# Forming weight sums two steps ahead, beside another block's products

## The chip, the cores and the metric

The kernel runs on one core of a Trainium2 chip. Its time is device microseconds of one execution; the number to compare is the median of several runs. Engines are named as in the profile: PE is TensorE's matmul, PEld its weight load, DVE VectorE, ACT ScalarE, POOL GpSimd, SP SyncE, which here issues nearly all DMA transfers.

## The reference

Retention (linear attention with a decay for each head) is followed by a layer of two matrix products with an activation between them. Batch 8, 8 heads, 576 positions, head size 64; the result of the attention, 4608 tokens x 512, goes through weights of 512 x 2048 and 2048 x 512, all in float32.

```python
scores = (q @ k.T) / sqrt(64)                  # per batch and head
ret = scores * where(i >= j, gamma[h] ** (i - j), 0)
x = (ret @ v).transpose(0, 2, 1, 3).reshape(4608, 512)
h = x @ w_in                                   # first products
g = h - tanh(h)
out = g @ w_out                                # second products
```

## The kernel before, in words

The sequence is cut into 9 chunks of 64 positions. A chunk of all 8 batches is a block of 512 columns (block n is chunk n). The attention of a block works in pairs of batches, with a running state for each batch and head, in small 64x64 matmuls. The 2048 middle features are 16 slices `f` of 128.

Every float32 operand of a large product is split in two words, a high word that ACT makes by rounding (`gh`, `xh`, `wi` and so on, in the type fp32r) and a low word that DVE makes by subtracting the high one (`gl`, `xl`). A product is then three matmuls: high x high, high x low, low x high. A first product of one slice is 12 matmuls (`mm1`, line 434), and so is a second product of one slice (`mm2`, line 489).

The order of work:

- Blocks 0 and 1 do their first products while the weights are being loaded and split. Their h goes to DRAM (`spill`).
- The late loop (line 686) does the second products of block 1 and then of block 0, 31 steps of 12 matmuls in the loop and one behind it. In step k, `words` splits g of step k + 1 (ACT `gh` at line 471, DVE `gl` at line 472), `resume` makes g of step k + 2 (ACT tanh at line 464, DVE subtraction `s` at line 465), and `fetch` loads step k + 4 from DRAM. In steps 3, 16 and 29 `entry3` does attention for block 2; it is followed by loads of its next operands on SP and their scaling on POOL (`prep`, line 240). Steps 7 and 20 have such a load and scaling too.
- Block 2 does its first products (line 972), its g going to DRAM by `spill`, and then its second products (`stage_b`), between which stands the attention of blocks 3 and 4 (`attend`).
- Blocks 3 to 8 go in pairs. For the two blocks of a pair and two slices f1, f2 of the first weights, eight half products are made from seven by a scheme of sums and differences (`stage_a`, `product`). The seven operands on the weights' side, variants 0 to 6 for each of 8 pairs j of slices, lie in DRAM (`wvar`, 56 entries of 256 KB). Three of them (0, 5, 6) are parts of the weights as they are, the raw words; four (1 to 4) are sums and differences, which `variants(j)` makes: four operations on POOL (lines 835 to 839), then on DVE ta (line 840) and tb (line 841), a cast of each on ACT (line 843), a low word of each on DVE (line 844) and two stores on SP (line 845).

`attend` (line 766) has its matmuls write the attention of two batches to the PSUM bank `own`, and makes from it the words of the seven operands on the side of x. `put(v, b, src, 0)` is a high word on ACT (line 760), `put(v, b, src, 1)` a low word on DVE (line 762). For the first block of a pair ACT also copies the bank to `a` in SBUF (line 790), for the second block to `own` in SBUF (line 802).

Each engine carries out its instructions in the order of the program (`in_order`); nothing is moved by a planner. A buffer with one tag is reused in turn; `xh1` and `xl1` are the words of x of block 1, which nothing reads once its first products are done. `xl1` also holds the result of block 1 on its way out in step 15 of the late loop. g has three buffers, `gh` and `gl` two each, `own` one bank.

Of the kernel before, what the change touches and what calls it, by code (L numbers as in the profile page):

```python
# [9 lines left out]
F32 = mybir.dt.float32  # L10
F32R = mybir.dt.float32r
# [3 lines left out]
ALU = mybir.AluOpType  # L15
# [4 lines left out]
P = 128  # L20
NF = DF // P
# [14 lines left out]
NV = 7  # L36
# [35 lines left out]
def retention_ffn(ctx: ExitStack, tc: tile.TileContext, ins, out, spill, wvar):  # L72
    nc = tc.nc
    first_d, krows_d, qkv_d, w_in, w_out, qtab_d, vtab_d, mask_d, decay_d = ins

    const = ctx.enter_context(tc.tile_pool(name="const", bufs=1))
    pool = ctx.enter_context(tc.tile_pool(name="pool", bufs=2))
# [7 lines left out]
    win, wout, wraw, masks = {}, {}, {}, {}  # L85

    def place(t, f):
        return "wi1" if (t, f) == ("i", 14) else f"w{t}{f}"
# [141 lines left out]
    def prep(j, t, n=2):  # L230

        if j >= NI:
            return
        c = j // B
        a = parts[j, t][:, :, 0]
        if t == 0:
            table = qtabs[c].unsqueeze(1).broadcast_to([P, n, 4, C])
        else:
            table = vtab[:, c].unsqueeze(1).unsqueeze(3).broadcast_to([P, n, 4, D])
        nc.gpsimd.tensor_tensor(a, a, table, op=ALU.mult)  # L240
# [86 lines left out]
    def bank(name, tag):  # L327
        return psp.tile([P, 2, 4, D], F32, tag=tag, bufs=2 if tag == "h" else 1, name=name)
# [5 lines left out]
    def pair(what, j, bank):  # L334
        return what(j, bank[:, 0]) + what(j + 1, bank[:, 1])
# [121 lines left out]
    def fetch(n, f):  # L457
        fetched[n, f] = pool.tile([P, BLK], F32, tag="g", bufs=3, name=f"s{n}_{f}")
        nc.sync.dma_start(fetched[n, f], spill[n, f])

    def resume(n, f):
        g = fetched[n, f]
        th = pool.tile([P, BLK], F32, tag="cv", bufs=4, name=f"th{n}_{f}")
        nc.scalar.activation(th, g, AF.Tanh)
        nc.vector.tensor_tensor(g, g, th, op=ALU.subtract)

    def words(n, f):
        g = fetched.pop((n, f))
        gh = pool.tile([P, BLK], F32R, tag="gh", name=f"gh{n}_{f}")
        gl = pool.tile([P, BLK], F32R, tag="gl", name=f"gl{n}_{f}")  # L470
        nc.scalar.copy(gh, g)
        nc.vector.tensor_tensor(gl, g, gh.bitcast(F32), op=ALU.subtract)
        gs[n, f] = (gh, gl)
# [110 lines left out]
    for j in range(B):  # L584
        o = psp.tile([P, 8, C], F32, tag=("o2", "o3", "own")[j % 3], bufs=1, name=f"own_first{j}")[:, :4]
# [50 lines left out]
    for k, (n, f) in enumerate(seq):  # L636
# [32 lines left out]
        if k in early:  # L669
            p = early[k]  # L670
# [8 lines left out]
    def raw_words(f):  # L679

        j, w = f // 2, win[f].bitcast(F32)
        for v, cc in ((0, 0), (5, 2)) if f % 2 == 0 else ((6, 2),):
            nc.sync.dma_start(wvar[:, NV * j + v].rearrange("p (s m) -> p s m", s=2), w[:, :, cc : cc + 2].rearrange("p s c m -> p s (c m)"))

    rest = []
    for k, (n, f) in enumerate(late):
        if k in (3, 16, 29):
            follow = entry3(first + (0, 2, 5)[(3, 16, 29).index(k)], rest)
        if 0 < k < len(late) - 1:
            words(*late[k + 1])  # L690
        if k < len(late) - 2:
            resume(*late[k + 2])
        if k + 4 < len(late):
            fetch(*late[k + 4])
        if k in (3, 16, 29):

            follow()
        if k in (7, 20):
            load_part(rest[0], 0)
            prep(rest.pop(), 0)  # L700
        if k >= NF:
            raw_words(k - NF)
        for _ in range(2 if k < 4 else 1):
            step()
        if k < len(late) - 1:
            mm2(n, f)
# [2 lines left out]

    turns = [(c + u) * B + b for c in range(FIRST, NC, 2) for b in range(0, B, 2) for u in range(2)]  # L710
    work = pool.tile([P, 4, DM], F32, tag="xl1", bufs=1, name="work")

    def place_of(f):
        return place("i", f) if f != 1 else "wi14"

    def load_tables(c):

# [38 lines left out]
    def put(v, b, src, sub):  # L756

        hi, lo = [x[:, :, b * C : (b + 2) * C].rearrange("p i (u t) -> p u i t", u=2) for x in xv[v]]
        if sub == 0:
            nc.scalar.copy(hi, src)  # L760
        else:
            nc.vector.tensor_tensor(lo, src, hi.bitcast(F32), op=ALU.subtract)  # L762
# [3 lines left out]
    def attend(m, between):  # L766

        j = turns[m]
        c, b = divmod(j, B)
        first, states = (c - FIRST) % 2 == 0, c < NC - 1  # L770
        if first and b == 0:
            new_xv()
        o = bank(f"own{j}", "own")
        outs, same = pair(m_out, j, o), []
        if states:
            new = bank(f"new{j}", "new")
            same += pair(m_state, j, new)
        more = m + 1 < len(turns)
        if more:
            sc = bank(f"s{turns[m + 1]}", "h")  # L780
            same = pair(m_score, turns[m + 1], sc) + same
        run(same, outs)
        if more:
            after_score(turns[m + 1], sc, 2)
        if first:
            a = pool.tile([P, 2, 4, C], F32, tag="cv", bufs=4, name=f"xa{j}")
            kept[b] = a
            put(0, b, o[:, :, 0:2], 0)
            put(5, b, o[:, :, 2:4], 0)
            nc.scalar.copy(a, o)  # L790
            if states:
                add_state(j, new)
            between()
            put(0, b, o[:, :, 0:2], 1)
            put(5, b, o[:, :, 2:4], 1)
        else:
            a = kept.pop(b)
            t13 = pool.tile([P, 2, 2, 2, C], F32, tag="cv", bufs=4, name=f"t13_{j}")
            t24 = pool.tile([P, 2, 2, 2, C], F32, tag="cv", bufs=4, name=f"t24_{j}")
            t1, t3, t2, t4 = t13[:, 0], t13[:, 1], t24[:, 0], t24[:, 1]  # L800
            own = pool.tile([P, 2, 4, C], F32, tag="cv", bufs=4, name=f"xb{j}")
            nc.scalar.copy(own, o)
            put(4, b, o[:, :, 2:4], 0)
            nc.vector.tensor_tensor(t3, own[:, :, 2:4], own[:, :, 0:2], op=ALU.subtract)
            nc.gpsimd.tensor_tensor(t2, t3, a[:, :, 0:2], op=ALU.add)
            nc.vector.tensor_tensor(t1, own[:, :, 0:2], a[:, :, 0:2], op=ALU.subtract)
            nc.gpsimd.tensor_tensor(t4, a[:, :, 2:4], t2, op=ALU.subtract)
            if states:
                add_state(j, new)
            put(3, b, t3, 0)  # L810
            put(2, b, t1, 0)
            between()
            put(4, b, o[:, :, 2:4], 1)
            put(3, b, t3, 1)
            put(2, b, t1, 1)
            put(1, b, t2, 0)
            put(6, b, t4, 0)
            put(1, b, t2, 1)
            put(6, b, t4, 1)
        prep_turn(m + 2, 0)  # L820
        prep_turn(m + 1, 1)
        load_turn(m + 3, 0)
        load_turn(m + 2, 1)


    def variants(j):

        f1, f2 = [win[2 * j + u].bitcast(F32) for u in range(2)]
        r1, r2, ta, tb = [pool.tile([P, 2, 2, P], F32, tag="cv", bufs=4, name=f"{n}{j}") for n in ("r1", "r2", "ta", "tb")]
        if j == 0:  # L830
            ots = [pool.tile([P, 2, 2, 2, P], F32R, tag="xh1", bufs=1, name=f"ot{j}_{u}") for u in range(2)]
        else:
            ots = [const.tile([P, 2, 2, 2, P], F32R, tag=place_of(2 * j - 2 + u), name=f"ot{j}_{u}") for u in range(2)]
        for r, f in ((r1, f1), (r2, f2)):
            nc.gpsimd.tensor_tensor(
                r.rearrange("p k c m -> p (k c) m"), f[:, 0], f[:, 1], op=ALU.add,
            )
        nc.gpsimd.tensor_tensor(ta[:, 1], r2[:, 0], r2[:, 1], op=ALU.add)
        nc.gpsimd.tensor_tensor(tb[:, 0], r1[:, 0], r2[:, 0], op=ALU.subtract)
        nc.vector.tensor_tensor(ta[:, 0], ta[:, 1], r1[:, 0], op=ALU.subtract)  # L840
        nc.vector.tensor_tensor(tb[:, 1], r1[:, 1], ta[:, 0], op=ALU.subtract)
        for u, t in enumerate((ta, tb)):
            nc.scalar.copy(ots[u][:, :, 0], t)
            nc.vector.tensor_tensor(ots[u][:, :, 1], t, ots[u][:, :, 0].bitcast(F32), op=ALU.subtract)  # L844
            nc.sync.dma_start(
                wvar[:, NV * j + 1 + 2 * u : NV * j + 3 + 2 * u], ots[u].bitcast(F32).rearrange("p v s c m -> p v (s c m)"),
            )

    slots = {}
    per = NV * NPAIR // 4  # L850
# [121 lines left out]
    for f in range(NF):  # L972
        mm1(2, f)
        if f == 0:
            mm2(*late[-1])
        if f % 2 == 1:
            variants(f // 2)
        if f == 8:
            load_turn(1, 0)
            load_turn(2, 0)  # L980
            load_turn(1, 1)
        if f == 11:
            prep_turn(1, 0)
# [68 lines left out]
```

## Time and profile before

| | us |
|---|---|
| median of 3 runs (884.51 to 888.09) | 887.48 |
| the profiled execution | 886.59 |
| its span | 884.8 |
| PE busy in the span | 851.0 |
| DVE busy | 491.2 |
| ACT busy | 340.6 |
| POOL busy | 188.2 |

Times in views of the trace are from the start of the span. In a row of the timeline come the start, the duration, the engine, the line, the operation, what it writes and reads, the shapes and the count of instructions merged; brackets give how long the engine stood idle before it and what ended that. Matmuls overlap: a row of four takes 1.07 us, but the next begins 0.91 us after it. A row of the list of waits says which engine at which line waited for which, the total, the number of times and the longest.

### The profile page before, as it was taken

Reading aid. Unit: us, or ns where it says so; the run is one execution under the profiler, and the core shown is the slowest. Engines: PE = TensorE matmul, PEld = TensorE weight load, DVE = VectorE, ACT = ScalarE, POOL = GpSimd, SP = SyncE. Lnnn points to the kernel's source line nnn. Section 1 sums busy time; section 2 is a strip of 40 time slices with the busy share of each in tenths; the row PEclk is TensorE's granted clock in tenths of the full one; section 3 lists DMA queues with packets and bytes.
Section 4 is the critical chain, followed back from the end, with each engine's and each line's share of the span. In section 5 each row is a group of like instructions: output and inputs, shape, how many; then the busy total and the mean of one; then the engine's idle time right before and its main releaser. Section 6 shows DMA issues by size and latency. Waiting matters only on the chain.

```text
span 884.8 us, 18546 instructions
## 1 busy us (share of the span) xinstructions
PE 851.0 (96%) x7701; PEld 699.6 (79%) x7702; DVE 491.2 (56%) x742; ACT 340.6 (38%) x633; POOL 188.2 (21%) x165
## 2 busy tenths in 40 slices
PE   7999999999786999999999999999999999999997
PEld 6788888878664777888888878888887888888886
DVE  5899876544575576544445766344447744343421
ACT  5887754443233232322233333222233333232221
POOL 0000001010673243211132343121115312121100
PEclk9999999999897999999999999999999999999999
DMA  8967945586588747644467646444476445442442
GB/s 319 365 232 252 350 137 179 164 294 199 183 300 312 282 144 213 206 166 143 167 206 221 219 164 213 161 163 146 167 238 199 139 134 174 169 153 109 118 122 71
DMA packets 72580, 174.54 MB, mean 197 GB/s; under 512 B 7472, under 2 KB 14896, under 8 KB 67120
## 3 DMA queue, kind: packets, MB, share of 16 engines
q1 hardware_dynamic: 71968, 172.44, 58.4%
q8 instruction: 60, 0.98, 0.4%
q10 hardware_dynamic: 528, 0.92, 0.3%
q14 instruction: 24, 0.20, 0.1%
HBM read 124.57 MB, written 48.76 MB: 196 GB/s over the span
## 4 chain that ended last, share of the span: by engine, by line
PE 84%; DMA 7%; DVE 4%; ACT 2%; issue 2%; POOL 0%; SPq 0%; ACTq 0%; DVEq 0%; POOLq 0%
PE o L489 25%; PE o L900 15%; PE h L434 12%; PE pnew L869 7%; PE pv L869 7%; PE pown L869 4%; PE py L869 4%; PE pz L869 4%; DMA s<-spill_dram 3%; PE own L290 3%; PE s L290 3%; PE new L290 2%; DMA spill_dram<-g 1%; DVE ot L844 1%; DMA qk<-in_qkv_dram 1%
## 5 line engine op out<-in xcount | busy, mean ns | idle before, releaser
L489 PE MATMUL o<-wo,gh 128*128 128x512 f32 x608 | 158.2, 398 | 8.5 <-ACT gh L884 7.6
L489 PEld LDWEIGHTS o<-wo,gh 128*128 128x128 f32 x608 | 113.8, 190 | 34.6 <-ACT gh L884 8.0
L923 POOL TENSOR_TENSOR c<-c,th 128x512 f32<-128x512 f32 x48 | 62.1, 1296 | 269.1 <-ACT th L919 267.9
L434 PE MATMUL h<-xh,wi 128*128 128x512 f32 x384 | 100.3, 397 | 9.0 <-DVE g L452 7.8
L919 ACT ACTIVATE th<-c 128x512 f32<-128x512 f32 x72 | 45.5, 632 | 148.5 <-DVE c L933 97.4
L434 PEld LDWEIGHTS h<-xh,wi 128*128 128x128 f32 x384 | 71.6, 190 | 27.4 <-DVE g L452 10.4
L489 PE MATMUL o<-wo,gl 128*128 128x512 f32 x304 | 85.0, 392 | 0.0
L900 PE MATMUL o<-wo,gs 128*128 128x512 f32 x288 | 70.6, 389 | 0.0
L240 POOL TENSOR_TENSOR vr<-vr,vtab 128x512 f32<-128x512 f32 x27 | 32.1, 1192 | 172.4 <-DMA vr<-in_qkv_dram 79.6
L489 PEld LDWEIGHTS o<-wo,gl 128*128 128x128 f32 x304 | 57.6, 190 | 12.2
L900 PEld LDWEIGHTS o<-wo,gs 128*128 128x128 f32 x288 | 54.1, 188 | 11.2
L290 PE MATMUL own<-qk,state 64*64 64x64 f32 x928 | 57.6, 221 | 3.1 <-DVE xlv L762 3.1
L869 PE MATMUL pnew<-xhv,ws 128*128 128x512 f32 x192 | 59.5, 391 | 0.3
L489 PE MATMUL o<-wo,gs 128*128 128x512 f32 x240 | 59.2, 394 | 0.0
L869 PE MATMUL pv<-xhv,ws 128*128 128x512 f32 x192 | 59.1, 389 | 0.0
L290 PE MATMUL own<-qk,vr 64*64 64x64 f32 x928 | 56.6, 219 | 1.0 <-issue 1.0
L434 PE MATMUL h<-xl,wi 128*128 128x512 f32 x192 | 52.4, 395 | 0.0
L885 DVE TENSOR_TENSOR gl<-s,gh 128x512 fp32r<-128x512 f32 x44 | 32.0, 733 | 36.8 <-ACT gh L884 24.9
L929 DVE TENSOR_TENSOR work<-pown,work 128x512 f32<-128x512 f32 x24 | 16.6, 690 | 64.5 <-PE pown L869 64.5
L489 PEld LDWEIGHTS o<-wo,gs 128*128 128x128 f32 x240 | 44.3, 188 | 9.6
L290 PEld LDWEIGHTS own<-qk,state 64*64 64x64 f32 x928 | 46.8, 134 | 3.8 <-ACT gh L884 1.9
L900 PE MATMUL o<-wo,gh 128*128 128x512 f32 x192 | 48.9, 389 | 0.0
(150 smaller groups left out, 1610.9 us busy)
## 6 DMA issues: line engine op xcount, KB each, us to landing
ws<-wvar_dram SPq DMA_DIRECT2D x42, 1024.0 KB, 4.9
s<-spill_dram SPq DMA_DIRECT2D x94, 256.0 KB, 3.8
qk<-in_qkv_dram SPq DMA_DIRECT2D x29, 512.0 KB, 4.7
vr<-in_qkv_dram SPq DMA_DIRECT2D x29, 512.0 KB, 5.6
spill_dram<-c SPq DMA_DIRECT2D x48, 256.0 KB, 2.2
spill_dram<-g SPq DMA_DIRECT2D x36, 256.0 KB, 4.0
rwi<-in_w_in_dram SPq DMA_DIRECT2D x16, 512.0 KB, 5.6
rwo<-in_w_out_dram SPq DMA_DIRECT2D x16, 512.0 KB, 5.4
```

The costliest lines, as they stand in the source:

```text
L240: nc.gpsimd.tensor_tensor(a, a, table, op=ALU.mult)
L290: nc.tensor.matmul(out_, w, x, start=start, stop=stop)
L434: nc.tensor.matmul(hp, win[f][:, a, cc, :], x[:, cc, :], start=(k == 0), stop=(k == 3 * NCC - 1))
L489: nc.tensor.matmul(ops[n][t], g[:, t * P : (t + 1) * P], wout[f_][:, a, :], start=(f_ == first and k == 0), stop=(f_ == final and k == 2),)
L844: nc.vector.tensor_tensor(ots[u][:, :, 1], t, ots[u][:, :, 0].bitcast(F32), op=ALU.subtract)
L869: nc.tensor.matmul(into, w[:, a, k], x[:, k], start=start and i == 0, stop=i == len(terms) - 1, skip_group_check=not start,)
L885: nc.vector.tensor_tensor(gl, g, gh.bitcast(F32), op=ALU.subtract)
L900: nc.tensor.matmul(ops[n][t], g[:, t * P : (t + 1) * P], wout[f][:, a, :], start=(j == 0 and f == fs[0] and k == 0), stop=last_,)
L919: nc.scalar.activation(th, c, AF.Tanh)
L923: nc.gpsimd.tensor_tensor(c, c, tanh(c), op=ALU.subtract)
L929: nc.vector.tensor_tensor(u2, y, u2, op=ALU.add)
```

## The change

Three things are changed.

1. The sums of the weights move from the first products of block 2 (a call behind every second slice) to the late loop. Each pair is made in two parts: `variants(j)`, the four POOL operations, in step k of `starts` = 1, 4, 8, 11, 16, 19, 22, 25, and `variants_out(j)`, the rest, in step k + 2. The intermediate sums now lie in one tile in `xl1` and the words in one tile in `xh1`.
2. The stores of the raw words move from the late loop's second half to the first products of block 2, one call for each slice.
3. In `attend` the low words of three operands are made from the copies in SBUF and no longer from the bank.

```diff
+    def place_of(f):
+        return place("i", f) if f != 1 else "wi14"
+
+    temps = {}
+    starts = (1, 4, 8, 11, 16, 19, 22, 25)
+
+    def variants(j):
+        f1, f2 = [win[2 * j + u].bitcast(F32) for u in range(2)]
+        temps[j] = pool.tile([P, 4, 2, 2, P], F32, tag="xl1", bufs=1, name=f"vt{j}")
+        r1, r2, ta, tb = [temps[j][:, u] for u in range(4)]
+        for r, f in ((r1, f1), (r2, f2)):
+            nc.gpsimd.tensor_tensor(r.rearrange("p k c m -> p (k c) m"), f[:, 0], f[:, 1], op=ALU.add)
+        nc.gpsimd.tensor_tensor(ta[:, 1], r2[:, 0], r2[:, 1], op=ALU.add)
+        nc.gpsimd.tensor_tensor(tb[:, 0], r1[:, 0], r2[:, 0], op=ALU.subtract)
+
+    def variants_out(j):
+        r1, r2, ta, tb = [temps[j][:, u] for u in range(4)]
+        ot = pool.tile([P, 4, 2, 2, P], F32R, tag="xh1", bufs=1, name=f"ot{j}")
+        nc.vector.tensor_tensor(ta[:, 0], ta[:, 1], r1[:, 0], op=ALU.subtract)
+        nc.vector.tensor_tensor(tb[:, 1], r1[:, 1], ta[:, 0], op=ALU.subtract)
+        for u, t in enumerate((ta, tb)):
+            at = ot[:, 2 * u : 2 * u + 2]
+            nc.scalar.copy(at[:, :, 0], t)
+            nc.vector.tensor_tensor(at[:, :, 1], t, at[:, :, 0].bitcast(F32), op=ALU.subtract)
+            nc.sync.dma_start(
+                wvar[:, NV * j + 1 + 2 * u : NV * j + 3 + 2 * u], at.bitcast(F32).rearrange("p v s c m -> p v (s c m)"),
+            )
+
     rest = []
     for k, (n, f) in enumerate(late):
...
-        if k >= NF:
-            raw_words(k - NF)
+        if k in starts:
+            variants(starts.index(k))
+        if k - 2 in starts:
+            variants_out(starts.index(k - 2))
         for _ in range(2 if k < 4 else 1):
             step()
...
             between()
-            put(0, b, o[:, :, 0:2], 1)
-            put(5, b, o[:, :, 2:4], 1)
+            put(0, b, a[:, :, 0:2], 1)
+            put(5, b, a[:, :, 2:4], 1)
...
-            put(4, b, o[:, :, 2:4], 1)
+            put(4, b, own[:, :, 2:4], 1)
...
-    def variants(j):
...
     for f in range(NF):
         mm1(2, f)
         if f == 0:
             mm2(*late[-1])
-        if f % 2 == 1:
-            variants(f // 2)
+        raw_words(f)
         if f == 8:
             load_turn(1, 0)
```

More of the change, by code (lines that the diff above doesn't have):

```diff
@@ L711, in retention_ffn @@
     work = pool.tile([P, 4, DM], F32, tag="xl1", bufs=1, name="work")
-    def place_of(f):
-        return place("i", f) if f != 1 else "wi14"
     def load_tables(c):
@@ L823, in attend @@
         load_turn(m + 2, 1)
-    def variants(j):
[L828 to L847, printed above, removed]
     slots = {}
```

## The prediction

> **What bounds the kernel now.** I began with the busy times cut by stage, since 96% of TensorE over the whole span hides the only question: in which stage does it stand still? The columns are stretch, length, then busy us of PE, PEld, DVE, ACT, POOL, granted clock, DMA share and GB/s.
>
> ```profile
> 119.20:167.70 48.50, 48.50 (x501) 40.37 (x503) 31.74 (x50) 23.80 (x42) 4.05 (x4) 1.00 0.40 123
> 167.70:213.30 45.60, 45.04 (x399) 36.78 (x389) 25.30 (x40) 18.88 (x34) 4.68 (x5) 1.00 0.87 278
> 213.30:271.20 57.90, 49.91 (x205) 38.95 (x203) 35.82 (x44) 17.72 (x32) 34.80 (x32) 0.94 0.63 223
> 271.20:349.50 78.30, 65.56 (x1217) 54.05 (x1218) 47.83 (x74) 25.75 (x57) 28.18 (x26) 0.93 0.69 240
> 469.60:533.10 63.50, 62.54 (x1218) 52.07 (x1218) 44.84 (x69) 23.36 (x53) 24.98 (x22) 1.00 0.64 203
> ```
>
> The second products of blocks 1 and 0 (the first two rows, the late loop) are TensorE solid. The first products of block 2 (third row) lose 8.0 us of idle and some clock. The second products of block 2 (fourth row) take 78.3 us, where the same work for block 4 (fifth row) takes 63.5. The change takes work out of rows three and four and puts it into rows one and two. Next, TensorE's own list of waits (us in total, times, longest), and its timeline at the holes:
>
> ```profile
> PE h L434 <- DVE g L452: 7.8, 4, 5.4
> PE o L489 <- ACT gh L884: 7.6, 1, 7.6
> PE own L290 <- DVE xlv L762: 3.1, 3, 1.4
> ```
> ```profile
> 232.43 2.07 PE L434 MATMUL h<-xh,wi 128*128 128x512 f32 x4 [5.36 <-DVE g L452]
> 234.30 1.91 PE L434 MATMUL h<-xl,wi 128*128 128x512 f32 x4
> ...
> 264.98 1.19 PE L434 MATMUL h<-xh,wi 128*128 128x512 f32 x4 [2.09 <-DVE g L452]
> ...
> 270.08 1.08 PE L434 MATMUL h<-xh,wi 128*128 128x512 f32 x4
> ...
> 281.72 3.78 PE L489 MATMUL o<-wo,gh 128*128 128x512 f32 x8 [7.55 <-ACT gh L884]
> ```
>
> All three waits are ones the diff aims at: DVE late with g behind the sums, the fetch of g late behind the sums' stores, and the bank `own` held by the low words.
>
> **Part 1, sums out of block 2: 10.5 us won.** A step of twelve matmuls takes 2.72 us: three of them lie between these rows of the late loop, (143.19 - 135.03)/3.
>
> ```profile
> 135.03 1.98 PE L489 MATMUL o<-wo,gh 128*128 128x512 f32 x8
> ...
> 143.19 1.98 PE L489 MATMUL o<-wo,gh 128*128 128x512 f32 x8
> ```
>
> The stretch holds 16 such steps and the last second product of block 0, so 17 x 2.72 = 46.2 of 57.9 us: 11.7 are lost. Without the sums DVE has one subtraction of 0.69 for each step, POOL nothing. What is late next is DMA: raw words (24 of 256 KB, 6 MB) replace sums (8 MB), with the same burst of loads at f = 8, and a spill's landing already reaches 8.7 us:
>
> ```profile
> DMA to landing us min/median/max: 2.0/3.7/8.7
> ```
>
> With three buffers a spill has about 3 x 2.72 = 8.2 us less the 1.3 of tanh and subtraction. I leave 1.2 us for that and take 10.5. Bounds: 6.0, if the spills hold up half of the steps as before, and 11.7.
>
> **Part 2, the way into the second products: 4.0 us won.**
>
> ```profile
> 272.00 1.66 SPq L453 DMA_DIRECT2D spill_dram<-g  x2
> 275.82 1.00 SPq L845 DMA_DIRECT2D wvar_dram<-ot  x2
> 276.91 2.30 SPq L459 DMA_DIRECT2D s<-spill_dram  x3
> ```
> ```profile
> 281.05 1.28 ACT L884 CAST gh<-s 128x512 fp32r<-128x512 f32 x2 [6.00 <-DMA s<-spill_dram]
> ```
>
> The last first product ends at 270.08 + 1.08 = 271.2. The fetch that TensorE then needs stands in SP's queue behind the last pair's stores, and is issued 5.7 us later. Now one raw word stands there, which waits for nothing: spill at +1.4, raw word to +2.3, fetch at +2.3. That is 3.4 us earlier; its landing (281.05 - 276.91 = 4.1) stays. TensorE's 7.55 idle becomes about 4.4, still long, so only about 0.6 of the slow clock behind it goes. Bounds 2 and 5.
>
> **Part 3, low words from SBUF copies: 1.6 us won.** The bank `own` comes free after ACT's copies, so the 3.1 us of waits for it go. But DVE's subtraction then has two SBUF operands, and those wait for POOL, as two group rows show (mean ns, 128x256) and one pair of instructions:
>
> ```profile
> L762 DVE TENSOR_TENSOR xlv<-t,xhv 128x256 fp32r<-128x256 f32 x48 | 47.7, 1050 | 0.0
> ...
> L762 DVE TENSOR_TENSOR xlv<-own,xhv 128x256 fp32r<-128x256 f32 x36 | 13.9, 413 | 0.0
> ```
> ```profile
> 211.40 1.04 POOL L240 TENSOR_TENSOR vr<-vr,vtab 128x512 f32<-128x512 f32 x1 [20.46 <-DMA vr<-in_qkv_dram]
> ```
> ```profile
> 211.48 1.50 DVE L472 TENSOR_TENSOR gl<-s,gh 128x512 fp32r<-128x512 f32 x1 [0.74 <-ACT gh L471]
> ```
>
> The subtraction that takes 0.69 alone took 1.50: it stood until POOL's multiply ended at 212.44. If all 36 moved subtractions rose to 1050 ns that is 36 x 0.64 = 23 us of DVE over three stages, some 8 in each, where DVE has 63.5 - 44.8 = 18.7 idle. At worst a tail of it delays `gl`; I take half of the 3.1, bounds -1 and 3.1.
>
> **Part 4, sums in the late loop: 17.9 us lost.** TensorE has nothing idle here, but ACT's and DVE's queues are in program order and carry its operand: `gh` (ACT) needs `s` (DVE), `gl` needs `gh`. Each round adds four POOL operations two steps ahead, then on DVE ta, tb and two low words, on ACT two casts, on SP two stores. The casts stand in front of the next `gh`. POOL's prices, and DVE's:
>
> ```profile
> 221.10 2.62 POOL L835 TENSOR_TENSOR r<-wi 128x512 f32<-128x512 f32 x2 [8.66 <-DMA out_dram<-ob]
> 223.80 0.74 POOL L838 TENSOR_TENSOR ta<-r 128x256 f32<-128x256 f32 x1
> ```
> ```profile
> 222.36 0.69 DVE L452 TENSOR_TENSOR g<-h,g 128x512 f32<-128x512 f32 x1 [2.72 <-ACT g L451]
> 224.57 0.42 DVE L840 TENSOR_TENSOR ta<-ta,r 128x256 f32<-128x256 f32 x1 [1.51 <-POOL ta L838]
> ```
>
> POOL: 2.62 + 2 x 0.74 = 4.1 us a round, and about 5.1 with two DVE operations of 0.5 let in between. What decides is when POOL may begin. In rounds 1, 2 and 4 its queue holds multiplies that wait for loads:
>
> ```profile
> 138.35 1.04 POOL L240 TENSOR_TENSOR vr<-vr,vtab 128x512 f32<-128x512 f32 x1 [58.39 <-DMA vr<-in_qkv_dram]
> ...
> 140.38 0.74 POOL L240 TENSOR_TENSOR one<-one,qtab 128x256 f32<-128x256 f32 x1
> 147.41 1.52 POOL L240 TENSOR_TENSOR qk<-qk,qtab 128x512 f32<-128x512 f32 x1 [6.29 <-DMA qk<-in_qkv_dram]
> 176.59 1.04 POOL L240 TENSOR_TENSOR vr<-vr,vtab 128x512 f32<-128x512 f32 x1 [27.66 <-DVE s L465]
> ...
> 178.80 0.74 POOL L240 TENSOR_TENSOR one<-one,qtab 128x256 f32<-128x256 f32 x1
> ```
> ```profile
> 133.82 0.39 SPq L212 DMA_DIRECT2D vr<-in_qkv_dram  x1
> 143.50 0.43 SPq L212 DMA_DIRECT2D qk<-in_qkv_dram  x1
> 170.86 0.86 SPq L212 DMA_DIRECT2D vr<-in_qkv_dram  x1
> ```
> ```profile
> 134.06 0.62 ACT L471 CAST gh<-s 128x512 fp32r<-128x512 f32 x1 [1.56 <-DVE s L465]
> ...
> 136.10 0.62 ACT L471 CAST gh<-s 128x512 fp32r<-128x512 f32 x1 [0.89 <-DVE s L465]
> ```
> ```profile
> 179.01 1.30 PE L489 MATMUL o<-wo,gh 128*128 128x512 f32 x5
> ```
>
> Step by step (k is the late loop's index; step 5 starts at 135.03, 8 at 143.19, 20 at 179.01):
> - Round 0, out at k = 3: DVE is full there (the `gh` at 134.06 waited for it) and ends 0.35 before step 5. ta and two casts push that `gh` by 1.45, so 1.1 late; POOL's four operations in the full stretch before hold at least one DVE operation (1.50 - 0.69 = 0.8). Late: 1.9.
> - Round 1, out at k = 6: POOL is free at 140.38 + 0.74 = 141.1, with the lateness 141.9; sums to 147.0; cast 147.6; `gh` of step 8 at 148.2 instead of 143.19. 5.0 in all, 3.1 more.
> - Round 2, out at k = 10: the load of qk stands on SP behind the stores of round 1 (low word at 148.4, `gl` of step 8 at 149.0, load at 149.5 instead of 143.50). Its multiply starts 3.9 later as now, 153.4, ends 154.7; sums to 159.8, two ACT casts of 0.62 to 161.0; step 12 was due at 148.2 + 4 x 2.72 = 159.1: 1.9 more.
> - Round 4, out at k = 18: step 16 starts 4 x 2.72 = 10.9 before step 20, at 168.1; POOL is free at 178.80 + 0.74 = 179.5, 11.4 later. Without raw words beside it vr lands 1.2 sooner (176.59 - 170.86 = 5.7 against 138.35 - 133.82 = 4.5): 10.2, sums to 15.3, cast and `gh` to 16.7. 5.8 more.
> - Rounds 3, 5, 6 and 7: POOL is free in time, but no lead is left. A round takes 2.1 of ACT's way (0.42 + 0.42 + 2 x 0.62) and 2.8 of DVE's (0.84 + 0.62 + 2 x 0.69), say 2.5, and 0.8 for one held operation. ACT and DVE can go at 2.04 a step (136.10 - 134.06), so they win back 0.68 of 2.72, 2.0 in three steps: 1.3 each, 5.2.
>
> Sum 1.9 + 3.1 + 1.9 + 5.8 + 5.2 = 17.9. Below: only rounds 1 and 4 bite, without interleaving (147.0 becomes 145.2, so 3.2; 4.8), with 1.5 for the rest: 9.5. Above: each round costs 3.1, 25.
>
> **The clock after a stop.** After 5.36 us idle the next eight matmuls took 2.07 + 1.91 instead of twice 1.08: 1.8 lost; after 2.09 idle, 1.19: nothing. My sum charges none behind the new stops, since ACT and DVE, not TensorE, are then last. The Trainium skill ("TensorE: Matmul & The Clock Gate", What's actually happening) has the array at half clock after about 3.4 us idle. By that rule the 5.8 us stop would cost up to 1.8 more, and the sum below would be 891.1; both rows agree with such a limit, and no run shown places it closer.
>
> **Sum.** -10.5 - 4.0 - 1.6 + 17.9 = +1.8. The profiled execution took 886.59 (span 884.8), 0.9 under the median of 887.48; so 888.4 for it, and 889.3 as a median.
>
> **Rivals.**
> - The queues' lead covers more (faster): `gh` runs up to 2.8 us ahead of TensorE once caught up, and POOL's turns fall in gaps. The late loop then costs its lower bound, 9.5: 887.5 - 16.1 + 9.5 = 880.9. For: DVE has 16.8 of 48.5 us idle in the first row. Against: the lead is gone exactly after the conversions and entries.
> - The late loop becomes bound by the ACT-DVE chain throughout (slower): each of eight rounds costs 3.1, 25 in all: 896.4. It decides beyond 0.5% from 2.6 us a round (20.5). For: 1.50 instead of 0.69 beside POOL. Against: 0.68 is won back in each step.
> - The sums leave block 2 but TensorE stays held there, by spills behind raw words (the change doesn't do what it says): Part 1 yields 6.0: 893.8. For: 0.87 DMA share beside raw words in the second row. Against: that stretch lost only 0.6.
>
> **How the numbers follow.** Forecast 0.38, chain 0.25, spills 0.10, faster 0.27. Half a per cent, 4.4 us, is about what a measurement can tell from no change. So faster 0.27, same 0.38, slower 0.35; the range reaches from a little under the first rival to beyond the second, 879 to 900; the forecast alone has 884 to 894.
>
> **What would show it.** Right: the late loop grows from 94.1 to about 112 us with TensorE waiting for `gh` at L471, worst at steps 8 and 20, DVE's ta waiting for POOL; block 2's first products shrink to about 47; the 7.55 wait falls to about 4.4; no wait for `own`. Wrong: a late loop under 105 or over 118, or block 2's first products above 51.

## The result and the profile after

The changed kernel takes 893.58 us (median of 10 runs, 891.88 to 894.62) where the kernel before, run beside it, takes 888.64 (10 runs, 884.51 to 893.10): a ratio of 1.0052, 95% interval 1.0034 to 1.0071. It is slower by half a per cent. The profiled execution has a span of 890.7 us, 5.9 more than before.

Where the 5.9 us come from is seen by cutting both traces at the same events. The late loop runs from its first second product to the first matmul of block 2; then come block 2's first products; "way" is the time from their end to the first second product of block 2; "second" goes to block 2's last second product, that is to the first `pnew`; "rest" is what follows it. The 119.2 us ahead of the late loop (119.3 after) are not in the table. All in us, each from the profiled execution.

| kernel | late loop | first | way | second | rest | span |
|---|---|---|---|---|---|---|
| before | 94.1 | 57.9 | 10.6 | 67.7 | 535.4 | 884.8 |
| changed | 116.7 | 48.4 | 7.3 | 64.6 | 534.5 | 890.7 |
| difference | +22.6 | -9.5 | -3.3 | -3.1 | -0.9 | +5.9 |

The windows cut at these events (columns: stretch, length, busy us of PE, PEld, DVE, ACT, POOL, granted clock, DMA share, GB/s); the first two are the late loop, cut at step 16:

```profile
119.30:180.80 61.50, 52.90 (x514) 40.87 (x512) 46.89 (x67) 28.09 (x50) 22.90 (x20) 0.97 0.49 164
180.80:236.00 55.20, 47.67 (x377) 37.52 (x373) 38.55 (x55) 22.52 (x41) 25.28 (x21) 0.94 0.59 193
236.00:284.40 48.40, 46.73 (x209) 38.13 (x211) 11.76 (x17) 10.15 (x17) 3.63 (x3) 1.00 0.77 254
284.40:356.20 71.80, 64.71 (x1216) 53.30 (x1217) 42.82 (x69) 24.30 (x55) 24.25 (x22) 0.95 0.71 241
```

The roles are exchanged: the third row, block 2's first products, is now solid (46.7 of 48.4 us), and the late loop, solid before, has TensorE idle for 16 us and a clock below 1. TensorE's waits, first one line of before, then those after, name who is late, and its timeline after shows the worst places:

```profile
PE o L489 <- ACT gh L471: 0.6, 2, 0.3
```
```profile
PE o L489 <- ACT gh L471: 15.5, 10, 6.1
PE o L489 <- ACT gh L890: 5.3, 1, 5.3
...
PE h L434 <- DVE g L452: 1.7, 1, 1.7
```
```profile
137.52 2.12 PE L489 MATMUL o<-wo,gh 128*128 128x512 f32 x8 [1.02 <-ACT gh L471]
...
150.25 3.61 PE L489 MATMUL o<-wo,gh 128*128 128x512 f32 x8 [4.16 <-ACT gh L471]
...
164.96 2.11 PE L489 MATMUL o<-wo,gh 128*128 128x512 f32 x8 [1.99 <-ACT gh L471]
...
198.06 3.59 PE L489 MATMUL o<-wo,gh 128*128 128x512 f32 x8 [6.09 <-ACT gh L471]
```

There are ten waits for `gh` where before there were two, of 0.3 us at most; the longest stand at steps 8 (150.25) and 20 (198.06). After these two the eight matmuls take 3.6 us instead of 2.1: a slow clock follows. How the longest wait comes about is read across three engines, POOL, DVE and ACT, at step 20:

```profile
189.43 1.04 POOL L240 TENSOR_TENSOR vr<-vr,vtab 128x512 f32<-128x512 f32 x1 [18.50 <-DMA vr<-in_qkv_dram]
...
192.07 2.48 POOL L697 TENSOR_TENSOR vt<-wi 128x512 f32<-128x512 f32 x2
194.63 0.72 POOL L698 TENSOR_TENSOR vt<-vt 128x256 f32<-128x256 f32 x1
```
```profile
195.38 0.93 DVE L705 TENSOR_TENSOR vt<-vt 128x256 f32<-128x256 f32 x1 [6.04 <-POOL vt L698]
```
```profile
196.35 1.14 ACT L709 CAST ot<-vt 128x512 fp32r<-128x512 f32 x2 [7.72 <-DVE vt L705]
197.39 0.61 ACT L471 CAST gh<-s 128x512 fp32r<-128x512 f32 x1
```

POOL stood 18.5 us for the load of vr; the sums came behind its scaling, DVE's ta waited 6.04 us for them, ACT's casts 7.72 us for ta, and `gh`, whose operand `s` had long been ready, stood behind the casts. Nothing in that chain except `gh` is needed by TensorE there.

### The profile page after: what moved, and what is told of

Its sections match the earlier page's. It is cut to its first block, busy times and chain, and to the rows that moved or that the text cites. A ratio compares the mean times of both kernels' runs of the same rounds, so it can differ in the third digit from the quotient of the medians.

```text
span 890.7 us, 18547 instructions
## 1 busy us (share of the span) xinstructions
PE 855.2 (96%) x7702; PEld 700.0 (79%) x7702; DVE 492.1 (55%) x742; ACT 339.5 (38%) x633; POOL 194.4 (22%) x165
## 4 chain that ended last, share of the span: by engine, by line
PE 82%; DVE 6%; DMA 4%; ACT 3%; POOL 2%; issue 2%; SPq 1%; DVEq 0%; POOLq 0%; ACTq 0%
PE o L489 22%; PE o L906 15%; PE h L434 12%; PE pnew L875 7%; PE pv L875 7%; PE py L875 4%; PE pown L875 4%; PE pz L875 4%; PE own L290 3%; PE s L290 2%; PE new L290 2%; DVE s L465 2%; DMA one<-in_qkv_dram 1%; POOL vt L697 1%; DMA spill_dram<-g 1%
## 5 line engine op out<-in xcount | busy, mean ns | idle before, releaser
L489 PE MATMUL o<-wo,gh 128*128 128x512 f32 x608 | 162.7, 406 | 21.3 <-ACT gh L471 15.5
L434 PE MATMUL h<-xh,wi 128*128 128x512 f32 x384 | 97.9, 392 | 2.8 <-DVE g L452 1.7
L434 PEld LDWEIGHTS h<-xh,wi 128*128 128x128 f32 x384 | 71.2, 188 | 19.1 <-DVE g L452 2.1
L290 PE MATMUL own<-qk,state 64*64 64x64 f32 x928 | 57.5, 221 | 0.0
L290 PE MATMUL own<-qk,vr 64*64 64x64 f32 x928 | 56.4, 219 | 0.8 <-issue 0.5
L906 PE MATMUL o<-wo,gh 128*128 128x512 f32 x192 | 48.9, 389 | 0.0
L290 PEld LDWEIGHTS own<-qk,vr 64*64 64x64 f32 x928 | 46.5, 135 | 1.1 <-issue 0.6
```

What stands on the lines that cost most here:

```text
L290: nc.tensor.matmul(out_, w, x, start=start, stop=stop)
L434: nc.tensor.matmul(hp, win[f][:, a, cc, :], x[:, cc, :], start=(k == 0), stop=(k == 3 * NCC - 1))
L489: nc.tensor.matmul(ops[n][t], g[:, t * P : (t + 1) * P], wout[f_][:, a, :], start=(f_ == first and k == 0), stop=(f_ == final and k == 2),)
L906: nc.tensor.matmul(ops[n][t], g[:, t * P : (t + 1) * P], wout[f][:, a, :], start=(j == 0 and f == fs[0] and k == 0), stop=last_,)
```

## The experiments

Three questions: what in the late loop costs the time, what the smaller parts are worth, and whether there is a better place. The ratios are to the kernel before, run on the same chip; the stage times are from the one profiled execution of each kernel. How far such a time varies by itself can be seen where the edits change nothing: in the kernels with the low words from SBUF the second products took 64.0 to 65.6 us.

| kernel | median us | ratio (95%) | late loop | first | way | second | span |
|---|---|---|---|---|---|---|---|
| scale_later | 887.80 | 1.0003 (0.9986 to 1.0020) | 110.8 | 48.3 | 6.9 | 64.0 | 885.5 |
| no_pool_sums | 874.29 | 0.9844 (0.9815 to 0.9873) | 97.9 | 48.3 | 7.3 | 64.1 | 872.8 |
| sums_unread | 891.66 | 1.0042 (1.0025 to 1.0059) | 116.7 | 47.6 | 6.8 | 64.1 | 889.7 |
| dve_sums_late | 884.00 | 0.9958 (0.9938 to 0.9979) | 107.2 | 47.8 | 7.2 | 64.1 | 880.2 |
| low_words_alone | 883.13 | 0.9948 (0.9931 to 0.9966) | 93.9 | 58.1 | 10.6 | 64.2 | 881.0 |
| low_words_psum | 899.00 | 1.0103 (1.0059 to 1.0147) | 116.6 | 47.8 | 6.9 | 71.9 | 898.9 |
| raw_in_late | 892.89 | 1.0061 (1.0040 to 1.0081) | 118.8 | 46.9 | 6.2 | 65.1 | 890.7 |
| dve_sums_block2 | 886.28 | 0.9986 (0.9967 to 1.0004) | 94.0 | 60.0 | 10.9 | 65.0 | 883.9 |
| split_pool | 890.86 | 1.0012 (0.9985 to 1.0038) | 105.7 | 54.9 | 6.2 | 64.8 | 887.0 |
| split_dve | 885.09 | 0.9971 (0.9957 to 0.9985) | 100.6 | 56.5 | 6.0 | 64.6 | 881.1 |
| one_tile | 881.29 | 0.9928 (0.9904 to 0.9952) | 94.3 | 54.2 | 10.6 | 65.6 | 879.2 |
| one_tile_early | 882.38 | 0.9926 (0.9905 to 0.9948) | 94.2 | 58.4 | 7.8 | 65.1 | 880.8 |

### What costs the time in the late loop

Two theories. A: POOL starts the sums late, behind scalings that wait for loads, and the lateness passes to `gh`. B: POOL holds up DVE while it works, wherever its operations stand.

**scale_later** takes the lateness away: the loads stay, but their scaling on POOL moves behind the sums of its neighbourhood.

```diff
-            prep(then, 1)
+            todo.append((then, 1))        # and so for the other scalings
...
+        if k in (6, 9, 18, 23, 29):
+            scale()                       # prep of all that stands in todo
```

> The changed kernel, with POOL's scaling of the attention's operands moved behind the sums of the weights in POOL's queue (steps 6, 9, 18 and 23 in place of 3, 7, 16 and 20); the loads stay where they are. Theory A (POOL starts the sums late in rounds 1, 2 and 4, because it stands at a multiply that waits for its load, and the queues of DVE and ACT stand behind the sums): the steps up to 8, 12 and 20 lose about 1.3 us each in place of 4.6, 3.8 and 6.3, the late loop falls from 116.7 to 103 to 106 us, and the time by 9 to 13 us, to 881 to 885. Theory B (the cost is the sharing of SBUF between POOL and DVE, and the added operations in the queues, all along): every sum still runs beside DVE, so the loop stays above 113 us and the time above 890.

```profile
PE o L494 <- ACT gh L476: 10.0, 15, 2.5
```

The line numbers stand five higher here. The long stops are gone (the longest wait is 2.5 us), and yet the late loop takes 110.8 us, between the ranges of the two theories: 5.9 won of the 22.6. Theory A is right for the two worst places, and not for the bulk.

**no_pool_sums** leaves POOL's four operations out; DVE, ACT and SP do all else that they do in the changed kernel, on the weights themselves.

```diff
-        for r, f in ((r1, f1), (r2, f2)):
-            nc.gpsimd.tensor_tensor(...)
-        nc.gpsimd.tensor_tensor(ta[:, 1], ...)
-        nc.gpsimd.tensor_tensor(tb[:, 0], ...)
```

> The changed kernel without POOL's four operations of each round; DVE's two, ACT's two casts, the two low words and the two stores stay, and read the weights themselves (so variants 1 to 4 are not the sums). Theory A: without POOL nothing makes DVE wait; what is left is the queue time of the added operations, hidden but for the full stretch in steps 3 to 5: late loop 96 to 100 us, time 873 to 879. Theory B, sharing part: the same low value, but then the kernel with later scaling stays high. Theory C (the added casts, subtractions and stores in the queues are the cost by themselves): late loop above 108 us, time above 885.

The late loop falls to 97.9. So eight rounds of ta, tb, casts, low words and stores cost 3.8 us, and the 32 operations of POOL cost the other 18.8.

**sums_unread** parts the two ways in which POOL can cost: its operations are back in their places, but nobody reads what they make.

> The kernel without POOL's operations, with them put back so that nobody reads their results: POOL makes the same four sums in the same places of its queue, but DVE's ta and tb, the casts and the stores still take the weights themselves (so the variants 1 to 4 are not the sums). What is left of POOL is its hold on DVE's two-operand subtractions; what is gone is any wait for its results. Theory A (the waits for POOL's late sums carry the loss): about 874 to 879, TensorE without stops over 2 us, the late loop at 98 to 102 us. Theory B (POOL holds DVE, and so delays `s` and `gl` and with them `gh`): 884 to 888, the late loop near the 110.8 of the kernel whose sums are never late.

The late loop takes 116.7 us, as long as in the changed kernel and longer than either theory had it. DVE has no wait for POOL there; it is held. Its timeline beside POOL's, in one stretch:

```profile
156.66 1.43 DVE L472 TENSOR_TENSOR gl<-s,gh 128x512 fp32r<-128x512 f32 x1 [0.74 <-ACT gh L471]
158.00 1.78 DVE L465 TENSOR_TENSOR s<-s,th 128x512 f32<-128x512 f32 x1
159.71 1.51 DVE L706 TENSOR_TENSOR vt<-wi,wi 128x256 f32<-128x256 f32 x1
...
162.02 2.89 DVE L711 TENSOR_TENSOR ot<-wi,ot 128x512 fp32r<-128x512 f32 x2
164.83 1.74 DVE L472 TENSOR_TENSOR gl<-s,gh 128x512 fp32r<-128x512 f32 x1
...
168.46 0.69 DVE L472 TENSOR_TENSOR gl<-s,gh 128x512 fp32r<-128x512 f32 x1 [0.74 <-ACT gh L471]
```
```profile
157.49 3.44 POOL L697 TENSOR_TENSOR vt<-wi 128x512 f32<-128x512 f32 x2
...
162.77 3.26 POOL L697 TENSOR_TENSOR vt<-wi 128x512 f32<-128x512 f32 x2
```
```profile
166.63 2.08 PE L489 MATMUL o<-wo,gl 128*128 128x512 f32 x4 [3.99 <-DVE gl L472]
```

The subtraction `gl` takes 0.69 us when POOL is still (168.46) and 1.4 to 1.8 beside it; so do `s` and the low words. In the late loops of no_pool_sums, changed, scale_later and sums_unread every `s` and `gl` that overlaps no POOL operation (161 of 240) took 0.68 to 0.70 us; the means of those that overlap one are 0.97, 1.20, 1.21 and 1.36. TensorE then waits 3.99 us for the `gl` that began at 164.83. How much DVE is held in all is seen from the late loop's windows of four kernels with the same 121 DVE instructions, no_pool_sums, changed, scale_later, sums_unread in this order:

```profile
120.26:218.17 97.91, 95.38 (x885) 76.61 (x885) 73.82 (x121) 50.26 (x91) 10.25 (x9) 1.00 0.63 213
```
```profile
119.27:236.00 116.73, 100.60 (x885) 78.42 (x884) 85.47 (x121) 50.61 (x91) 48.21 (x41) 0.96 0.54 178
```
```profile
120.33:231.14 110.81, 99.56 (x885) 75.63 (x884) 89.51 (x121) 50.48 (x91) 51.71 (x41) 1.00 0.57 187
```
```profile
119.44:236.17 116.73, 102.96 (x885) 79.82 (x884) 93.21 (x121) 50.60 (x91) 49.98 (x41) 0.94 0.53 178
```

DVE is busy for 73.8 us without POOL, and for 85.5, 89.5 and 93.2 with it: 11.7, 15.7 and 19.4 us are holds. In the changed kernel the hold is smallest, because DVE meanwhile waits for POOL's results, as the list of its waits has it:

```profile
DVE vt L705 <- POOL vt L698: 8.7, 3, 6.0
```

Hold and wait together are 20.4 there; in scale_later, with 2.0 of such waits, 17.7; in sums_unread 19.4. The late loop is longer than without POOL by 18.8, 12.9 and 18.8. Where no stop was over 2.5 us (scale_later), the 17.7 cost only 12.9, with a granted clock of 1.00; in the other two it was 0.96 and 0.94. So theories A and B are two faces of one thing: while POOL works on SBUF, DVE stands, either at its own subtractions or for POOL's result. The Trainium skill ("SBUF — State Buffer", SBUF: two separate sides) says that GpSimd and VectorE share one pair of ports under an exclusive lock, held for a whole instruction, against VectorE operations with two SBUF inputs beside a GpSimd operation that reads SBUF; the stretched rows agree.

**dve_sums_late** moves the same four operations to DVE.

```diff
-            nc.gpsimd.tensor_tensor(r..., f[:, 0], f[:, 1], op=ALU.add)
+            nc.vector.tensor_tensor(r..., f[:, 0], f[:, 1], op=ALU.add)   # and the other two
```

> The changed kernel with the four sums of each round on DVE instead of POOL, in the same places of the late loop. DVE gets 8 x (2 x 0.69 + 2 x 0.42) = 18 us, and without POOL beside it is not slowed. DVE had 57 us of the late loop's 94 busy, the rest of the sums brings it to 75, so it comes to some 93 of 98: nearly full. If a held DVE is what costs (theory B): the late loop at 100 to 106 us, 877 to 883. If it is the mere number of operations in front of `gh` on DVE and ACT (theory C): 888 or more, as with POOL.

```profile
118.99:226.22 107.23, 97.88 (x886) 76.27 (x884) 89.62 (x153) 50.35 (x91) 10.40 (x9) 1.00 0.59 193
```

With 32 instructions more DVE is busy for 89.6 us, 4.1 more than in the changed kernel, and the loop is 9.5 shorter: 107.2, just past the upper end of theory B's 100 to 106, at 884.0 us. 107.2 is still 9.3 over the loop without sums. DVE is busy for 84% of the loop, and TensorE's waits there are many and short (longest 1.95). Not all of it is the mere number of operations (theory C). The longest wait begins at a shared buffer: at k = 16 DVE stands 3.75 us until the result of block 1 has left `xl1`, into which the sums are to go, and the next `gl` stands behind the sums:

```profile
181.81 1.29 DVE L697 TENSOR_TENSOR vt<-wi 128x512 f32<-128x512 f32 x2 [3.75 <-DMA out_dram<-ob]
```
```profile
184.56 1.19 PE L489 MATMUL o<-wo,gl 128*128 128x512 f32 x4 [1.95 <-DVE gl L472]
```

With the two waits that follow it, of 0.96 and 0.62, that is up to 3.5 of the 9.3 us. How the rest divides between the added operations and other causes was not tried.

### What the smaller parts are worth

**low_words_alone** is the kernel before with the third part of the change alone.

```diff
-            put(0, b, o[:, :, 0:2], 1)
+            put(0, b, a[:, :, 0:2], 1)      # and so for 5 (from a) and 4 (from own)
```

> The kernel before, with only the low words of x from the SBUF copies. The prediction's step: the waits for the bank own (3.1 us) go, half of it is given back by DVE standing behind POOL: 1.6 us faster (ratio 0.998), bounds 1 slower and 3.1 faster. Rival: wholly given back, ratio 1.000 to 1.001, with the waits turned into waits for gl.

It is faster (0.9948), and its span is 3.8 us shorter, more than the upper bound of 3.1 set for it. By stage the gain is in block 2's second products alone, 67.7 to 64.2. There the waits for `own` behind a low word are gone (two of 1.4), against new ones of 0.5 and 0.2 for POOL. Another 0.8 us lies before the attention: 24 matmuls behind the long stop took 8.35 us before (281.72 to 290.07) and 7.53 here, the slow clock having ended sooner; nothing in the trace ties that to the edit. The remaining 0.6 is not placed. The group of low words from `xa` keeps 416 ns, those from `xb` take 1192, and no TensorE wait comes of it:

```profile
L762 DVE TENSOR_TENSOR xlv<-xb,xhv 128x256 fp32r<-128x256 f32 x12 | 14.3, 1192 | 0.0
...
L762 DVE TENSOR_TENSOR xlv<-xa,xhv 128x256 fp32r<-128x256 f32 x24 | 9.0, 416 | 0.0
```

None of the 24 from `xa` overlaps a POOL operation, and all 12 from `xb` do, so only a third of the moved subtractions can pay the hold.

**low_words_psum** is the changed kernel without that part.

> The changed kernel with the low words read from PSUM again, as before. If the 3.5 us that the copies gained alone are theirs here too, block 2's second products go from 64.5 to about 67.7 us and the time to 896 to 897. If they gained only beside the old sums: 893, as the changed kernel.

It is slower than the changed kernel, 899.0 (4 runs, 894.8 to 900.7; the profiled one is the longest), and above both expected values. Its second products take 71.9, 7.3 more: 1.65 is the wait for `own` again; 2.06 is one for `gh`, behind a fetch that landed late (ACT's cast waited 11.5 us for it), and 2.06 one for a scaled qk. Whether the low words bring those two about was not shown.

**raw_in_late** is the changed kernel with the raw words stored in the late loop's second half again.

```diff
+        if k >= NF:
+            raw_words(k - NF)
...
-        raw_words(f)                        # block 2
```

> The changed kernel with the stores of the raw words back in the second half of the late loop. If the raw words in block 2 cost only the spill that came late (1.7 us) and the one store in front of the fetch (about 1 us): block 2's first products 46.5 to 47 us, the wait behind them about 4.4. In the late loop theory A has the loads of round 4 land 1 to 1.5 us later behind the raw words, so the stop at step 20 grows by as much and the loop to 117.5 to 119 us: time 891 to 894, no clear difference. Rival (DMA share is what counts): loop above 121 us, time above 896.

The late loop becomes 2.1 us longer, block 2's first products and the way 1.4 and 1.1 shorter, and the span is the same. Where the raw words stand costs next to nothing either way.

### A better place

**dve_sums_block2** (low words from SBUF, sums in block 2 as before, but on DVE) takes POOL out of the sums without moving them.

> The kernel before with the low words from SBUF, and the four sums on DVE instead of POOL, left in block 2's first products. It tells the engine from the place. If POOL beside DVE is what held block 2's first products back, their 58 us fall to about 50, the way into the second products stays at 10.6, and the time is 873 to 877. If the stores' waits in SP's queue hold them, they stay at 56 to 58 and the time at 881 to 884.

The first products take 60.0 us instead of 58.1, so taking POOL out does not free block 2. It doesn't show that POOL's holds cost nothing there: DVE has the sums to do as well (42.2 us busy in that stage instead of 35.7), and a stop of 4.66 us stands at the same step as the 5.35 before. The following runs lead to the cause of that stop.

**split_pool** and **split_dve** leave the sums of pairs 0 to 3 in block 2 (after f = 1, 4, 7, 10) and put those of pairs 4 to 7 into the late loop at k = 8, 11, 22, 25, on POOL and on DVE.

```diff
+    starts = (8, 11, 22, 25)
...
+        if k in starts:
+            late_sums(4 + starts.index(k))
+        if k - 2 in starts:
+            late_out(4 + starts.index(k - 2))
...
-        if f % 2 == 1:
-            variants(f // 2)
+        if f in (1, 4, 7, 10):
+            variants(f // 3)
```

> Low words from SBUF; the sums of half the pairs stay in block 2's first products (rounds after f = 1, 4, 7 and 10, so that no pair's stores stand ahead of the fetch), those of the other half lie in the late loop at k = 8, 11, 22 and 25, away from the conversions and entries; raw words in the late loop as before. Reckoned by stage from the kernel before (884.8): block 2's first products 58 to 50 or less, the way to the second products 10.6 to about 6.5, second products -3.5. In the late loop POOL costs 1.6 us a round where its results are never late (12.9 for eight), so +6.5 for four and +1 for what is not POOL: span about 877, time 878 to 882. If a round's price is set by the place (those rounds without a stop in the changed kernel were free), the late loop stays under 97 and the time is 874 to 876.

> The same with the sums in the late loop on DVE. With eight rounds there DVE cost 9.3 us more than no sums at all, 1.2 a round, but nearly all of its stops were at k = 5 to 8 and 16 to 19, where no round lies now. So 0 to 0.6 a round: the late loop at 95 to 98, span 871 to 874, time 873 to 877, no slower than the same with POOL.

Both took longer than expected. Four rounds cost 11.6 us in the late loop on POOL (105.7) and 6.5 on DVE (100.6), about half of what eight cost there, so the places chosen were no cheaper; and block 2 with half the sums kept most of its loss (54.9 and 56.5). The second point was the useful one: a stop of 4.3 or 5.3 us stood at the same step as before, although the second round of sums now came a step later. Its cause stands in the trace of the kernel before, on ACT:

```profile
225.03 0.62 ACT L843 CAST ot<-ta 128x512 fp32r<-128x512 f32 x1 [2.70 <-DVE ta L840]
230.44 0.62 ACT L843 CAST ot<-tb 128x512 fp32r<-128x512 f32 x1 [4.79 <-DMA wvar_dram<-ot]
230.96 1.08 ACT L451 ACTIVATE g<-h 128x512 f32<-128x512 f32 x2
```

For the first pair the two results `ot` share one buffer (`xh1`). The cast of tb waits 4.79 us until the store of ta has left it, and the tanh of the next two steps stand behind the cast.

**one_tile** gives them one tile with two halves.

```diff
-            ots = [pool.tile([P, 2, 2, 2, P], F32R, tag="xh1", bufs=1, ...) for u in range(2)]
+            both = pool.tile([P, 4, 2, 2, P], F32R, tag="xh1", bufs=1, name="ot0")
+            ots = [both[:, 2 * u : 2 * u + 2] for u in range(2)]
```

> The kernel with the low words from SBUF alone, and one edit: the first pair's two results `ot` lie in one tile instead of two that share one buffer. In the chain of waits behind the 5.35 us stop in block 2's first products, ACT's cast of tb waits 4.8 us until the store of the first result has left that buffer, and the tanh for the next step stands behind the cast. If that wait makes the stop (theory D: the loss that the change moved out of block 2 was mostly one buffer, not the sums), the stop and the slow clock behind it go: first products 58.1 to 51 to 53, the rest as it was, span 874 to 876, time 876 to 879. If the sums' work holds block 2 (theory E, the reading of the prediction's first part), the stop only moves to another step: 56 to 58, 881 to 884.

```profile
226.30 0.62 ACT L844 CAST ot<-tb 128x512 fp32r<-128x512 f32 x1 [0.42 <-DVE tb L842]
```
```profile
225.25 0.96 DVE L842 TENSOR_TENSOR tb<-r,ta 128x256 f32<-128x256 f32 x1
226.14 1.78 DVE L845 TENSOR_TENSOR ot<-ta,ot 128x512 fp32r<-128x512 f32 x1
227.84 1.75 DVE L845 TENSOR_TENSOR ot<-tb,ot 128x512 fp32r<-128x512 f32 x1
229.51 1.28 DVE L452 TENSOR_TENSOR g<-h,g 128x512 f32<-128x512 f32 x2
```
```profile
230.25 1.19 PE L434 MATMUL h<-xh,wi 128*128 128x512 f32 x4 [2.94 <-DVE g L452]
```

The cast waits 0.42 instead of 4.79, the stop falls from 5.35 to 2.94, and the first products from 58.1 to 54.2: 3.9 us by one small edit, where the whole change takes 9.5 out of that stage. The rest of the stop is again a hold: tb and the two low words in front of g take 0.96, 1.78 and 1.75 us, together 2.7 more than alone. So both theories have a part: D for 3.9 us, and E, by these holds, for what is left of this stop. How the other 5.8 us between 54.2 and the changed kernel's 48.4 divide was not shown. The 54.2 lies between the ranges of the two, the time, 881.29 us (0.9928), in that of E. It is the lowest median of these kernels with all sums made, but the interval overlaps that of low_words_alone: the span is only 1.8 shorter than there, since the second products took 1.4 and the late loop 0.4 longer, about as much as stage times vary by themselves.

**one_tile_early** makes each round two steps earlier, so that no pair's stores stand ahead of the fetch.

```diff
-        if f % 2 == 1:
-            variants(f // 2)
+        if f == 0 or f % 2 == 1 and f < NF - 1:
+            variants((f + 1) // 2)
```

> The same with every round of sums two steps earlier (pair 0 after f = 0, pair j after f = 2j - 1, the last after f = 13), still on POOL in block 2, so that no pair's stores stand ahead of the fetch. By the gap of the changed kernel (7.3 us where 10.6 were before) it gains 3 to 3.5 us on the kernel with one tile: span 870 to 873, time 873 to 876. If the raw words and not the place of the last stores had shortened that gap, it stays at 10.6, and the time equals that of the one tile alone.

The way falls from 10.6 to 7.8 us, nearly as expected, 2.8 won by the place of the last stores alone, with raw words in the late loop. But with two rounds in the first two steps the first products are back at 58.4, and the time is that of one_tile, 882.38 (0.9926), and not the 873 to 876 expected. Rounds at f = 1, 3 and on, with only the last ones early, weren't tried.

## Why the prediction was right, and where its terms were off

The time, 893.6, lies 4.3 above the 889.3 forecast and inside the range. The direction was right and the size too small: +1.8 us was forecast, the medians differ by 4.9 and the profiled spans by 5.9. "Same" was given 0.38 and "slower" 0.35, parted at half a per cent; the interval of the ratio, 1.0034 to 1.0071, lies on both sides of it, so which of the two came true is open. The signs named for a right account were seen: `gh` is what TensorE waits for in the late loop, worst at steps 8 and 20, DVE's ta waits for POOL, and no wait for `own` behind a low word is left.

- **Part 1** (-10.5): measured -9.5. The first products fell to 48.4, against the forecast 47; one wait of 1.67 us for g is left. The size was right, its reason only in part: the sums were blamed as work in front of g, and one_tile shows that 3.9 us came from a buffer with one owner, which a wait of ACT in the trace of before had named. The one_tile trace shows the rest of that stop as holds.
- **Part 2** (-4.0): measured -3.3 in the way, where 3.4 of it was forecast. The other 0.6 was for the slow clock behind the stop; the first 24 matmuls there took 8.10 us and before 8.35, so 0.25. The fetch is issued at 288.14, 3.8 us after the last first product's end (283.30 + 1.07) and not 2.3:

```profile
286.13 1.91 SPq L683 DMA_DIRECT2D wvar_dram<-wi  x1
288.14 1.38 SPq L459 DMA_DIRECT2D s<-spill_dram  x3
```

  The one raw word ahead of it took SP 1.91 us to issue; from the spill's issue (285.75, as forecast 1.4 after the end) to the fetch's it was 2.4 us, where 0.9 had been allowed. Its landing was quicker than before (ACT's cast began at 290.98, 2.8 later, not 4.1). So the two errors nearly cancel, which is luck. The stop itself is 5.3 instead of the forecast 4.4 and the former 7.55: before, the attention's matmuls ahead of it waited 0.9 us behind POOL's last sums (`PE s L290 <- POOL ta L838: 0.9, 1, 0.9`), and without that wait it begins sooner.
- **Part 3** (-1.6, bounds to 3.1): measured -3.1, of which 0.25 is the clock of part 2, and -3.5 alone, of which 0.8 is the clock. The hold that had been subtracted hit only the `xb` third and delayed nobody. The term was mis-sized; half of the waits was given away without a row that asked for it.
- **Part 4** (+17.9): measured +22.6. The start of steps in both traces gives the rounds. Before, steps 12 and 16 start at

```profile
154.07 1.29 PE L489 MATMUL o<-wo,gh 128*128 128x512 f32 x5
```
```profile
168.00 2.11 PE L489 MATMUL o<-wo,gh 128*128 128x512 f32 x8
```

  and after, step 16 starts at 180.79 and block 2 at 236.00 (213.31 before):

| step | before | after | late in all | added since | forecast |
|---|---|---|---|---|---|
| 5 | 135.03 | 137.52 | 2.5 | 2.5 | 1.9 (round 0) |
| 8 | 143.19 | 150.25 | 7.1 | 4.6 | 3.1 (round 1) |
| 12 | 154.07 | 164.96 | 10.9 | 3.8 | 1.9 (round 2) |
| 16 | 168.00 | 180.79 | 12.8 | 1.9 | 1.3 (round 3) |
| 20 | 179.01 | 198.06 | 19.1 | 6.3 | 5.8 (round 4) |
| block 2 | 213.31 | 236.00 | 22.7 | 3.6 | 3.9 (rounds 5 to 7) |

  The places are as foretold, worst at steps 8 and 20 by POOL's late start. By the table every round up to 20 cost 0.5 to 1.9 more, the slow clock of the next point included. In round 1 POOL's two additions began at 143.43 (forecast 141.9) and with DVE in between took 2.98; DVE's `s` beside them took 1.58 instead of 0.69. One held operation of 0.8 us a round had been allowed. The windows give 11.7 us of holds over eight rounds, 1.5 a round.
- **The clock after a stop**, charged at nothing, cost twice 1.6 us: the steps behind the stops of 4.16 and 6.09 lasted from 150.25 to 154.62 and from 198.06 to 202.41, 4.4 us instead of 2.72. These 3.3 us of the 22.6 lie in the lines of step 12 and of block 2; without them round 2 cost 2.2 (forecast 1.9) and rounds 5 to 7 together 2.0 (forecast 3.9), so that the last line fits is luck. "ACT and DVE, not TensorE, are then last" did not hold: once `gh` was there, TensorE was.

Of the rivals, the chain that would bind the late loop throughout came nearest in its own terms: 22.6 us is 2.8 a round, above the 2.6 from which it was said to decide. But without the clock it is 2.4, and the rounds are uneven, so the chain did not bind throughout; sums_unread shows, though, a held DVE costing as much with no wait for a sum at all. Spills holding block 2 did not happen (third window: 46.7 of 48.4 us busy), though 893.8 was that rival's time: the number agrees, the mechanism does not. Less lead covered than the faster rival needed: `gh` was late in ten steps.

## What to carry to other kernels

Before work is moved into a stretch where TensorE never waits, count what its neighbours in the same queues will be held for: here four POOL operations, together some 4 us, cost DVE 1.5 us of holds a round beside the waits for their results. An engine that looks 40% idle by its own busy time took on its own share of the sums for 3.8 us of the loop, but could not take the holds on top. Before a stage's loss is put down to its amount of work, follow the longest stop back to the one wait that starts it: removing a wait of 4.8 us behind a shared buffer took 3.9 us out of the stage and cost the late loop nothing that can be told from noise, where the whole move took out 9.5 and cost 22.6.

## What the runs showed of the hardware

The clock fell after shorter stops than expected. In the 4 us after a stop the granted clock was 1.00 in the first row below (scale_later, a stop of 2.46 us), and 0.57 in the second (dve_sums_block2, 2.65 us):

```profile
192.58:196.58 4.00, 3.08 (x13) 2.24 (x13) 3.26 (x4) 1.22 (x3) 3.37 (x3) 1.00 0.85 306
```
```profile
265.54:269.54 4.00, 4.00 (x11) 3.16 (x12) 3.47 (x8) 0.91 (x3) 0.00 (x0) 0.57 0.89 349
```

Of the 46 stops over 1.5 us between 115 and 310 us of the 14 traces all 30 of 2.65 us or more were followed by a slow clock (0.50 to 0.64 in these 4 us), and the 16 of 2.46 or less were not, but for two of 1.62 and 1.93 (and after one of 2.06 it fell 4 us later). What sets these three apart was not found. Four us at 0.59 lose 1.6. The Trainium skill ("TensorE: Matmul & The Clock Gate", What's actually happening) puts the fall after an idle window of about 3.4 us; the measured stops of 2.65 and 2.94 are shorter, so the measurement decides: here stops up to 2.46 us mostly cost no clock, and none of 2.65 us or more went without.
